# All tiles behind w_out lie 64 bytes further in SBUF, and the led expert's first-layer results begin at the first byte of their tiles

## The chip, the cores and the metric

The kernel runs on one core of one Trainium2 chip. The metric is the device time of one execution in microseconds (us). A core has five engines with queues of their own: TensorE (PE in the rows; its weight loads are listed as PEld), VectorE (DVE), ScalarE (ACT), GpSimd (POOL) and SyncE (SP, which here issues most DMAs). SBUF is the on-chip memory of 128 partitions; a tile has an address, the same in every partition, and the addresses below are bytes within a partition. PSUM takes the results of TensorE.

## The reference

```python
attn = sm_attn(mean4(q), mean4(k), mean4(v)) repeated 4x  +  local attention, |i - j| < 4    # 4 x 8 heads x 576 x 64
x = attn as [2304, 512]
h = maximum(maximum(x @ w1, x @ w2), x @ w3)          # [2304, 768]
x = h @ w_out                                         # [2304, 512]
e = argmax(x @ w_gate); g = softmax(x @ w_gate)[e]    # 8 experts, one per token
out = g * (relu(x @ W1[e]) @ W2[e])                   # 512 -> 1024 -> 512
```

## The kernel before

Every large product is made of three matmuls on parts: each operand is split into a high part (rounded to fp32r) and a low part (the rest), and high x high, low x high and high x low are accumulated in PSUM. The parts lie in SBUF as tiles of their own.

**Stages.** (1) Attention, in 16 units of two heads, to about 165 us; its results are the blocks `xb`, nine blocks of 256 tokens in four rotating tiles, each with a high and a low half. (2) The dense layers, block by block: `mul` (L1011, results `hp`) multiplies the weights w1, w2, w3 (stationary, 128x128 each, tiles `w{h,l}{n}`, shown as wh and wl) with `xb` (moving, 256 columns); 18 groups of 12 matmuls a block, 216 in all. The maximum of three goes to `ht` (tag `hT`, two rotating tiles). Then `mul_out` (L1039, results `yp`) multiplies `ht` (stationary) with `w_out` and the gate's columns (moving, 260 of 520 columns a matmul; tiles woh and wol); 72 matmuls a block. (3) Experts. The expert with most tokens (the led expert) is done in seven blocks of 256 tokens: `m1_led` (L1580, results `ehp`) has the expert's first layer as stationary operand, three of four parts in tiles of the tag `xb` (`ew1`), the fourth in pages that held w1 to w3 (`eh`, `el`), and the gathered tokens `xT` (tile `xL`) as moving operand; 96 matmuls a block. `relu_led` (L1592 on ScalarE, L1594 on VectorE) writes the results in two parts to two tiles `ehT` of the tag `hT`. `m2_led` (L1604, results `eo`) has `ehT` as stationary and the second layer `W2`, in pages, as moving operand, 512 columns; 48 matmuls a block. The other experts' full slots of 128 tokens follow: `m1` (L1687) with xT stationary and the first layer moving, `hte`, which writes `ehT` tiles of [128, 2, 8, 128] of the same tag `hT`, and `m2` (L1727), again `ehT` stationary and `W2` moving. The rests of fewer than 128 tokens (`racc`, L1849) are interleaved.

**Order of work.** A planner (`Plan`) with costs written by hand sets the order of every engine's instructions when the program is built. It knows durations and buffers, but no addresses.

**Where tiles lie.** Pools are stacks: a tag gets its place at its first `pool.tile`, in the order of the program, rounded up to 32 bytes. In the pool `main` these are the 18 weight pages of 4096 bytes, `lg` (576), the tag woh and the tag wol (12,480 bytes each, the size of the w_out tiles that take the place of `raw` and `tmp`), four tiles of the tag `xb` (8192 each), two of the tag `hT` (12,288 each), `hf`, `ys`. Behind `main` lies the pool of attention, and later in its place the pool `rt` of the experts (with `xL`). The identity `C["ident"]` lies in a pool ahead of `main`.

Of the kernel before, what the change touches and what calls it, by code (L numbers as in the profile page):

```python
# [10 lines left out]
F32 = mybir.dt.float32  # L11
F32R = mybir.dt.float32r
# [18 lines left out]
LED = 14  # L31
TB = 256
NB = NT // TB
OFF = 16
WIN, KW = 58, 64
NW = 10
CUT = (0, S // 2, S)
# [93 lines left out]
class Plan:  # L131
# [10 lines left out]
    def __init__(s, stock, fill=None, turns=()):  # L142
        s.fill, s.load, s.seen, s.cols = fill, 0.0, 0.0, [{} for _ in range(2)]
        s.stock = {k: [0.0] * n for k, n in stock.items()}
        s.jobs, s.free, s.port, s.turn, s.n = [], {}, 0.0, {t: [] for t in turns}, 0
# [134 lines left out]
class Attention:  # L280
# [36 lines left out]
    def bank(s, shape, name):  # L317
        return s.psum.tile(shape, F32, name=name, tag="at", bufs=4)
# [420 lines left out]
class Dense:  # L739


    def __init__(s, nc, pool, psum, ws, wo, wg, y, C):
        s.nc, s.pool, s.psum, s.ws, s.wo_d, s.wg_d, s.y, s.C = nc, pool, psum, ws, wo, wg, y, C
        s.hid, s.hp, s.hf, s.yp, s.ys, s.last, s.jl, s.js = {}, {}, {}, {}, {}, {}, [], []
        s.w = [[pool.tile([128, 2, 4, 128], F32R, name=f"w{i}", tag=f"w{i}{n}") for n in range(9)] for i in "hl"]
        s.xb = {}
        s.lg = pool.tile([128, NTL, E], F32, name="lg")
        s.ht, s.read = {}, {}

        s.raw = pool.tile([128, 3, 4, 128, 2], I32, name="raw", tag="woh")  # L750
        s.tmp = pool.tile([128, 3, 4, 128], F32, name="tmp", tag="wol")

    def bank(s, n, name):
        return s.psum.tile([128, n], F32, name=name, tag="mm", bufs=4)
# [305 lines left out]
class Experts:  # L1060
# [524 lines left out]
    def relu_led(s, f, part):  # L1585
        nc, t = s.nc, s.hp["led", f]
        if f + part == 0 and "led" not in s.hT:
            h = [s.pool.tile([128, OFF + 2048], F32R, name="ehT", tag="hT", bufs=2) for _ in range(2)]
            s.hT["led"] = [x[:, OFF:].rearrange("p (f t) -> p f t", f=8) for x in h]
        h, l = (x[:, f] for x in s.hT["led"])  # L1590
        if part == 0:
            nc.scalar.activation(out=h, in_=t, func=ACTF.Relu)  # L1592
        else:
            nc.vector.scalar_tensor_tensor(  # L1594
                out=l, in0=t, scalar=0.0, in1=h.bitcast(F32), op0=ALU.max, op1=ALU.subtract,
            )
# [433 lines left out]
```

## Time and profile before

| | |
|---|---|
| runs before | 696.35 us median of 3 (695.89 to 697.23) |
| profiled execution | 698.38 us, of which the span from the first to the last instruction is 696.5 us |
| PE busy | 680.4 us, 98% of the span |
| DVE, ACT, POOL busy | 346.1, 275.4, 126.7 us |
| granted TensorE clock | 0.995 of full speed as a mean |

Busy time of PE counts overlapping matmuls once; a matmul's own duration is longer than the distance from its start to the next start, because they are pipelined. The distance is read from how many matmuls begin in a stretch in which PE has no gap.

### The profile page before, as it was taken

To read this page: it belongs to the slowest core of one execution; us is meant where nothing else is said; L and a number is where in the kernel's file an instruction comes from. 1 tells how busy PE (TensorE), PEld (TensorE's weight loads), DVE (VectorE), ACT (ScalarE), POOL (GpSimd) and SP (SyncE) were. 2 spreads that over 40 slices of the span, in tenths; PEclk is the share of its full clock that TensorE was granted. 3 is DMA by queue.
4 is the path that set the end of the run, shared out by engine and by line. 5 is a ranking of instruction groups with operands and counts; after the bars stand their busy time and mean duration, and the time that the engine had idled before them with its cause. 6 is when DMAs were issued, how large, how long until landed. Compare 5 with 4: busy or idle time off the path is not lost.

```text
span 696.5 us, 15470 instructions
## 1 busy us (share of the span) xinstructions
PE 680.4 (98%) x6135; PEld 604.9 (87%) x6143; DVE 346.1 (50%) x849; ACT 275.4 (40%) x799; POOL 126.7 (18%) x148
## 2 busy tenths in 40 slices
PE   8898999999999999999999999999999999999996
PEld 4565799999999999999999999899898798787775
DVE  5989976796444472231222227864121121146863
ACT  3764656676453362222111112621221222237752
POOL 2436432302310020100000000412121211201111
PEclk9999999999999999999999999999999999999999
DMA  7756524334331110101000003605125343354640
GB/s 243 239 162 222 196 68 117 117 102 138 116 104 38 48 38 2 48 1 48 2 32 16 16 16 103 232 32 163 65 82 192 106 135 123 111 192 159 205 140 32
DMA packets 32241, 73.12 MB, mean 105 GB/s; under 512 B 4319, under 2 KB 4575, under 8 KB 32160
## 3 DMA queue, kind: packets, MB, share of 16 engines
q1 hardware_dynamic: 26528, 57.63, 25.7%
q0 software_dynamic: 3040, 9.70, 4.2%
q10 hardware_dynamic: 2592, 4.72, 1.9%
q8 instruction: 50, 0.82, 0.5%
q14 instruction: 31, 0.25, 0.1%
HBM read 75.18 MB, written 9.70 MB: 122 GB/s over the span
## 4 chain that ended last, share of the span: by engine, by line
PE 88%; DVE 5%; DMA 4%; issue 1%; SPq 1%; ACT 0%; POOL 0%; POOLq 0%; DVEq 0%; ACTq 0%
PE hp L1011 30%; PE ehp L1580 11%; PE yp L1039 11%; PE eo L1604 11%; PE eo L1727 3%; PE ehp L1687 3%; PE racc L1849 2%; PE tp L363 2%; PE to L568 1%; PE xtp L1672 1%; PE ts L398 1%; PE td L479 1%; PE tz L540 1%; DMA eh<-in_moe_w_dram 1%; PE tt L513 1%; DMA xg<-y,r_go 1%
## 5 line engine op out<-in xcount | busy, mean ns | idle before, releaser
L1011 PE MATMUL hp<-xb,wh 128*128 128x256 f32 x1296 | 230.8, 282 | 0.0
L1011 PEld LDWEIGHTS hp<-xb,wh 128*128 128x128 f32 x1296 | 196.2, 188 | 2.0 <-issue 0.8
L1011 PE MATMUL hp<-xb,wl 128*128 128x256 f32 x648 | 180.1, 278 | 0.0
L1011 PEld LDWEIGHTS hp<-xb,wl 128*128 128x128 f32 x648 | 121.9, 188 | 0.0
L1021 DVE TENSOR_TENSOR hf<-hf,hp 128x256 f32<-128x256 f32 x108 | 45.2, 419 | 93.3 <-PE hp L1011 91.6
L1594 DVE SCALAR_TENSOR_TENSOR ehT<-ehp,ehT 128x256 fp32r<-128x256 f32 x56 | 23.7, 424 | 114.1 <-ACT ehT L1592 113.9
L1604 PE MATMUL eo<-eh,ehT 128*128 128x512 f32 x224 | 69.9, 393 | 0.0
L1039 PE MATMUL yp<-woh,ht 128*128 128x260 f32 (+1 forms) x408 | 69.4, 290 | 0.0
L1580 PE MATMUL ehp<-xT,ew 128*128 128x256 f32 x504 | 68.7, 282 | 0.0
L1580 PEld LDWEIGHTS ehp<-xT,ew 128*128 128x128 f32 x504 | 63.1, 189 | 3.5 <-ACT ob L1739 1.7
L1024 ACT CAST ht<-hf 128x256 fp32r<-128x256 f32 x54 | 22.0, 407 | 94.4 <-DVE hf L1021 94.0
L1039 PEld LDWEIGHTS yp<-woh,ht 128*128 128x128 f32 x408 | 57.0, 188 | 1.0
L1604 PEld LDWEIGHTS eo<-eh,ehT 128*128 128x128 f32 x224 | 41.5, 188 | 10.7 <-issue 0.8
L1657 POOL DMA_INDIRECT xg<-y,r_go x14 | 17.6, 1254 | 165.8 <-DMA eh<-in_moe_w_dram 120.9
L1592 ACT ACTIVATE ehT<-ehp 128x256 fp32r<-128x256 f32 x56 | 21.5, 385 | 60.3 <-PE ehp L1580 60.3
L1604 PE MATMUL eo<-el,ehT 128*128 128x512 f32 x112 | 43.7, 390 | 0.0
L1039 PE MATMUL yp<-wol,ht 128*128 128x260 f32 (+1 forms) x204 | 43.2, 288 | 0.0
L1744 POOL DMA_INDIRECT out_dram<-ob,r_si x18 | 19.1, 1062 | 113.7 <-ACT ob L1739 101.9
L1739 ACT ACTIVATE ob<-eo,r_ga 128x512 f32<-128x512 f32 x17 | 11.7, 688 | 65.3 <-PE eo L1604 33.2
L1039 PEld LDWEIGHTS yp<-wol,ht 128*128 128x128 f32 x204 | 31.9, 188 | 0.5
L1028 DVE TENSOR_TENSOR ht<-hf,ht 128x256 fp32r<-128x256 f32 x54 | 23.6, 436 | 14.5 <-ACT ht L1024 14.1
L1018 ACT COPY hf<-hp 128x256 f32<-128x256 f32 x54 | 20.1, 372 | 25.6 <-PE hp L1011 25.5
(272 smaller groups left out, 1145.2 us busy)
## 6 DMA issues: line engine op xcount, KB each, us to landing
rw<-in_moe_w_dram SPq DMA_DIRECT2D x64, 256.0 KB
eh<-in_moe_w_dram SPq DMA_DIRECT2D x20, 512.0 KB
el<-in_moe_w_dram SPq DMA_DIRECT2D x20, 512.0 KB
raw<-in_moe_w_dram SPq DMA_DIRECT2D x18, 512.0 KB
vb<-in_vs_dram SPq DMA_DIRECT2D x16, 320.0 KB
qt<-in_q_dram SPq DMA_DIRECT2D x16, 288.0 KB
kt<-in_k_dram SPq DMA_DIRECT2D x16, 288.0 KB
vr<-in_v_dram SPq DMA_DIRECT2D x16, 288.0 KB
```

The lines of the kernel that those rows point to most:

```text
L1011: s.nc.tensor.matmul(t, s.part(a, m, g)[:, kk], s.xb[j][:, x, kk], start=n == 0, stop=n == 11)
L1018: s.nc.scalar.copy(out=s.hf[j, m], in_=s.hp.pop((j, m, 0)))
L1021: s.nc.vector.tensor_tensor(out=s.hf[j, m], in0=s.hf[j, m], in1=s.hp.pop((j, m, g)), op=ALU.max)
L1024: s.nc.scalar.copy(out=s.ht[j][:, 0, m], in_=s.hf[j, m])
L1028: s.nc.vector.tensor_tensor(out=h[:, 1, m], in0=s.hf.pop((j, m)), in1=h[:, 0, m].bitcast(F32), op=ALU.subtract)
L1039: s.nc.tensor.matmul(p, s.ht[j][:, a, kk, ts], s.wo[w][:, kk, c0:c1], start=kk + i == 0, stop=kk + i == 7)
L1580: s.nc.tensor.matmul(t, s.W1[j][a][:, f * 128:(f + 1) * 128], s.xL[:, x, j], start=n == 0, stop=n == 11,)
L1592: nc.scalar.activation(out=h, in_=t, func=ACTF.Relu)
L1594: nc.vector.scalar_tensor_tensor(out=l, in0=t, scalar=0.0, in1=h.bitcast(F32), op0=ALU.max, op1=ALU.subtract,)
L1604: s.nc.tensor.matmul(s.op[k, 0], h[a][:, j, i * 128:(i + 1) * 128], s.second(b, j), start=j == 0 and w == 0, stop=j == 7 and w == 2,)
L1687: s.nc.tensor.matmul(s.hp[k][f], a[:, j], s.W1[j][b][:, f * 512:(f + 1) * 512], start=j == 0 and w == 0, stop=j == 3 and w == 2,)
L1727: s.nc.tensor.matmul(s.op[k, cols.start], a[:, j], s.second(b, j, cols), start=j == 0 and w == 0, stop=j == 7 and w == 2)
```

## The change

A tile of 16 fp32 (64 bytes) that nothing reads or writes is allocated in the pool `main` right behind woh and wol, so every tile allocated after it (xb, hT, hf, ys, and the pools of attention and `rt`) lies 64 bytes further. The two `ehT` tiles of the led expert lose the 16 fp32 ahead of their results: they become plain [128, 8, 256] tiles. `ehT` of the slots (`hte`) had no such offset and is not edited.

```diff
-OFF = 16
+SHIFT = 16
...
         s.raw = pool.tile([128, 3, 4, 128, 2], I32, name="raw", tag="woh")
         s.tmp = pool.tile([128, 3, 4, 128], F32, name="tmp", tag="wol")
+        pool.tile([128, SHIFT], F32, name="shift")
...
     def relu_led(s, f, part):
         nc, t = s.nc, s.hp["led", f]
         if f + part == 0 and "led" not in s.hT:
-            h = [s.pool.tile([128, OFF + 2048], F32R, name="ehT", tag="hT", bufs=2) for _ in range(2)]
-            s.hT["led"] = [x[:, OFF:].rearrange("p (f t) -> p f t", f=8) for x in h]
+            h = [s.pool.tile([128, 8, 256], F32R, name="ehT", tag="hT", bufs=2) for _ in range(2)]
+            s.hT["led"] = h
         h, l = (x[:, f] for x in s.hT["led"])
```

## Rows read from the trace of the kernel before

**Rows 1.** The page: span, busy time of each engine, granted clock in 40 slices.
```profile
span 696.5 us, 15470 instructions
...
PE 680.4 (98%) x6135; PEld 604.9 (87%) x6143; DVE 346.1 (50%) x849; ACT 275.4 (40%) x799; POOL 126.7 (18%) x148
...
PEclk9999999999999999999999999999999999999999
```

**Rows 2.** The page: the chain that ended last, by engine and by line.
```profile
PE 88%; DVE 5%; DMA 4%; issue 1%; SPq 1%; ACT 0%; POOL 0%; POOLq 0%; DVEq 0%; ACTq 0%
PE hp L1011 30%; PE ehp L1580 11%; PE yp L1039 11%; PE eo L1604 11%; PE eo L1727 3%; PE ehp L1687 3%; PE racc L1849 2%; PE tp L363 2%; PE to L568 1%; PE xtp L1672 1%; PE ts L398 1%; PE td L479 1%; PE tz L540 1%; DMA eh<-in_moe_w_dram 1%; PE tt L513 1%; DMA xg<-y,r_go 1%
```

**Rows 3.** Busy time in two stretches: length, engines (instructions), clock, DMA share, GB/s.
```profile
293.00:308.00 15.00, 15.00 (x130) 15.00 (x129) 4.65 (x11) 3.23 (x9) 0.00 (x0) 1.00 0.00 1
321.00:340.00 19.00, 19.00 (x170) 19.00 (x169) 5.92 (x14) 3.44 (x9) 0.00 (x0) 1.00 0.00 1
```

**Rows 4.** L1011, 293.1 to 308, then 321 to 340: duration ns least/median/most.
```profile
L1011 PE MATMUL hp<-xb,wl x43: 280/281/282, 292.9 to 307.7; 128*128 128x256 f32 x43
L1011 PE MATMUL hp<-xb,wl x57: 275/276/277, 320.9 to 339.9; 128*128 128x256 f32 x57
```

**Rows 5.** Groups, blocks at 76:115, 117:163, 196:228, 238:273, 282:310, 318:343 (busy, mean ns).
```profile
L1011 PE MATMUL hp<-xb,wl 128*128 128x256 f32 x71 | 19.9, 280 | 0.0
L1011 PE MATMUL hp<-xb,wl 128*128 128x256 f32 x72 | 20.0, 278 | 0.0
L1011 PE MATMUL hp<-xb,wl 128*128 128x256 f32 x70 | 19.5, 278 | 0.0
L1011 PE MATMUL hp<-xb,wl 128*128 128x256 f32 x71 | 19.8, 279 | 0.0
L1011 PE MATMUL hp<-xb,wl 128*128 128x256 f32 x72 | 20.2, 280 | 0.0
L1011 PE MATMUL hp<-xb,wl 128*128 128x256 f32 x72 | 19.9, 277 | 0.0
```

**Rows 6.** The chain in order of time: start us, us on the chain, what.
```profile
291.77 18.37 PE hp L1011 x156
...
318.76 24.50 PE hp L1011 x216
343.26 8.62 PE yp L1039 x72
...
468.63 5.48 PE eo L1604 x24
...
505.10 11.24 PE ehp L1580 x96
...
531.13 11.45 PE ehp L1580 x96
...
649.91 5.71 PE eo L1727 x24
...
663.23 5.59 PE eo L1727 x24
...
684.37 5.67 PE eo L1727 x48
```

**Rows 7.** L1604 over the span, then L1727 from 661 to 667: least/median/most ns.
```profile
L1604 PE MATMUL eo<-eh,ehT x224: 387/389/500, 468.4 to 632.2; 128*128 128x512 f32 x112
L1727 PE MATMUL eo<-eh,ehT x12: 397/397/398, 663.1 to 666.8; 128*128 128x512 f32 x12
```

**Rows 8.** Busy time in a stretch of L1604 and one of L1727, columns as above.
```profile
470.00:475.00 5.00, 5.00 (x30) 4.29 (x28) 4.93 (x9) 0.00 (x0) 2.73 (x3) 1.00 0.38 105
661.50:666.50 5.00, 5.00 (x23) 4.07 (x22) 4.72 (x5) 4.11 (x5) 0.00 (x0) 1.00 0.00 0
```

## The prediction

> **What bounds the kernel now.** I read the page first, then the chain, then stretches of TensorE. The page shows PE busy for 680.4 of 696.5 us, with the granted clock at full speed in all 40 slices [rows 1], and the chain that ended last is 88% PE, 30% of it the three-way first layer (hp, L1011) [rows 2]. So nearly every nanosecond by which one matmul follows another counts, and the question for a change that only moves tiles is whether that spacing depends on where tiles lie. The reader should see in the rows that it does.
>
> Compare two stretches of one instruction. From 293 to 308 us PE runs 130 hp matmuls, from 321 to 340 us 170 of the same shape [rows 3]. On the chain, 156 of them take 18.37 us in the block around the first stretch, 117.8 ns each; 216 take 24.50 us in the next block, 113.4 ns each [rows 6]. The single matmul shows it too: 281 ns in the first stretch, with nothing outside 280 to 282, and 276 in the second, with nothing outside 275 to 277 [rows 4]. In both stretches PE never waits, the granted clock is 1.00, the DMA share is 0.00, and VectorE and ScalarE do much the same (4.65 and 3.23 us of 15; 5.92 and 3.44 of 19) [rows 3]. So neither clock nor DMA nor the other engines make the difference; what is left is how the two operands of TensorE are read beside each other, a pattern that, once entered, holds for 17 us.
>
> The same stands between two lines of one shape. The 128x512 second layer takes 389 ns at its median over all seven blocks of the led expert (L1604), and 397, nothing outside 397 to 398, in the slots behind it (L1727) [rows 7]; on the chain 24 of them take 5.48 us and 5.59 to 5.71 us, 228 and 233 to 238 ns each [rows 6]. Both read W2 from the same pages as the moving operand and an ehT tile as the stationary one. VectorE is as busy in the fast stretch (4.93 of 5 us) as in the slow one (4.72) [rows 8]. What differs is the place: the led expert's ehT begins 64 bytes into its tile, that of the slots at the first byte.
>
> **Distances.** I count, for each pair, moving start minus stationary start, modulo 512 bytes (one stationary block is 128 columns of 4 bytes, and inside every tile named here but those of w_out the slices start at multiples of 512). From the shapes in the order of allocation: 18 weight pages of 4096 bytes, lg of 576, woh and wol of 12,480 each make 99,264 bytes from the first page to xb, 448 modulo 512; the four xb tiles of 8192 and a 12,288-byte hT tile keep that, so hT lies at 448 as well, and xL at 384. Hence now: hp (moving xb, stationary pages) 448; led eo 448 + 64, so 0; slots' eo (stationary at 448) 64; ehp (moving xL) 448 against ew1, which lies in xb tiles, and 384 against its fourth weight part, which lies in pages. The rows say: 0 is fast, 64 slow, 448 either, and ehp at 448 with 384 is slow most of the time (96 in 11.24 to 11.45 us, 117 to 119 ns each) [rows 6].
>
> **The change part by part.** It adds a 64-byte tile that no instruction reads or writes, and takes the led expert's own 64 bytes away. No instruction, wait, DMA or queue entry is added, removed or moved past another; the planner's order doesn't depend on addresses. So only spacing can change.
>
> *Led eo (L1604):* pages stay, and ehT stays as well (64 bytes of shift in place of 64 of offset), so 0 remains: no change.
>
> *hp (L1011):* xb moves by 64, pages don't, so 448 becomes 0, the distance of led eo. What this is worth: a slow hp matmul costs 117.8 - 113.4 = 4.4 ns. How many are slow I read from the mean duration of the low-part matmuls by block: 280, 278, 278, 279, 280 in the first five and 277, which stands for the last four (276 to 277) [rows 5]. Over 277 the five are 3 + 1 + 1 + 2 + 3 = 10 ns; a wholly slow block would be 4 over it, so 2.5 blocks of 216 matmuls are slow: 540 x 4.4 ns = 2.4 us. Counted over 276 with 5 ns for a slow block it is 18/5 = 3.6 blocks, 3.4 us; I take 2.6. The first two blocks hold 4 of the 10 ns, and there attention is interleaved and waits of other engines set part of the end; half of their 1.0 us is lost. That leaves 2.1 us. Bounds: a gain of 3.4 where all becomes fast and all is on the path; a loss where all becomes slow (below).
>
> *Slots behind the led expert (L1727, L1687):* hT moves against W2's pages, so 64 becomes 0. On the chain the x24 pieces of 5.71, 5.59 and a third like it become 24 x 227 ns = 5.45 (0.26 + 0.14 + 0.14), and the x48 piece of 256 columns, 5.67 us, becomes 48 x 113.4 = 5.44 (0.23) [rows 6]: 0.77 us, of which I take 0.6, since this tail also waits on splits of VectorE and ScalarE (4.72 and 4.11 of 5 us [rows 8]). Bounds 0 and 0.77. Their first layer keeps its distance in three of four parts: nothing.
>
> *ehp (L1580):* ew1 and xL both move, so 448 stays; against pages 384 becomes 448. A quarter of the matmuls gets another distance. If all 672 ran at 113.4 ns, a block of 96 would take 10.89 us in place of 11.24 to 11.45, and the seven blocks would give 3.4 us; if all ran at 117.8 they would lose 0.3. I take the quarter, 0.8.
>
> *yp (L1039):* ht moves by 64 against woh and wol. These rows are 520 columns, so the distances run through 24 values in steps of 16 bytes and all of them shift together. A block of 72 takes 8.62 us, 119.7 ns each [rows 6], as a mean over fast and slow places; shifting the set of places leaves a mean much as it is. I take 0; 1 ns either way over some 600 is 0.6 us.
>
> *Attention:* its tiles move together, and only pairs with the identity, which stays, change. I take 0, and 1 us either way: tp is the longest of these lines on the chain, 2% of 696 us [rows 2], and 4 ns in 113 of that is 0.5.
>
> *DMAs:* the same packets to places 64 bytes on; 0.
>
> [...]
>
> **Sum.** 2.1 + 0.6 + 0.8 = 3.5 us. Against the profiled execution, 698.38 us with a span of 696.5 [rows 1], that is 694.9. The median of the runs is 696.35, 2.0 us lower with the same program; a pattern that holds by chance could be in fewer blocks there, so I take off some of it: 3.1 us, 693.2.
>
> **Rivals.** *Nothing happens.* hp at the one distance 448 runs at both paces, so distance alone doesn't decide; what starts the slow pattern may be the entry into a block, and then it comes and goes at 0 as well, while gains in the slots are eaten by yp. For it: the two paces in one tile. Against: led eo, whose median is 389 through seven blocks with many entries [rows 7]. 696.35, chance 0.18.
>
> *Slower: hp locks into the slow pattern at 0.* The slots' eo shows that a distance can be slow throughout, and no row shows a 256-column matmul at 0. Place: L1011, nine blocks. Of 1944 matmuls some 590 are slow now (2.6 us / 4.4 ns); the other 1354 would cost 4.4 ns each, 6.0 us, less 1.4 from slots and ehp: 696.35 + 4.6 = 701.0. It decides from some 330 additional slow matmuls on (1.4 us). [...] Chance 0.10.
>
> *More: ehp, all of it at one distance, locks into the fast pattern*, as hp did in four blocks: 2.1 + 0.6 + 3.4 = 6.1 us, 690.2. For it: hp's late blocks at 448. Against: hp's first five blocks at 448. Chance 0.12.
>
> **How the numbers follow.** My forecast, hp fast nearly throughout, slots fast, ehp partly, has 0.60, and 691.8 to 695.4 of its own. A measurement of this kernel can tell some 0.2%, 1.4 us. Faster by more than that: 0.57 of the forecast and all of the larger gain, 0.69. Within: 0.18 and 0.03, 0.21. Slower: 0.10. The range reaches from the larger gain to somewhat above no change, with yp and attention against it: 690.0 to 697.6; outside are the slow lock and the tails.
>
> **What would show it.** Right: hp low-part matmuls at 276 to 277 ns in all nine blocks, no stretch at 281, x216 pieces of 24.5 us; L1727 at 389 in place of 397; L1604 unchanged at 389; yp still near 8.6 us per 72. Wrong: hp at 281 in stretches or throughout, L1727 still at 397 (then distance modulo 512 is the wrong measure), or yp pieces moved by more than 0.1 us each. If hp is fast everywhere and the time stands, the gain went into waits in the attention part, and PE's idle time there would show it.

## The result, and the profile after

The changed kernel takes 705.0 us, the median of 5 runs (703.3 to 705.67), against 696.35 us for the kernel before on the same chip (695.77 to 697.36). The ratio is 1.0118, with a 95% interval of 1.0101 to 1.0136: it is slower by 8.65 us. The forecast was 693.2 us; the range ended at 697.6. What came is the rival to which the prediction gave 0.10, hp in the slow pattern at distance 0, and 4.0 us beyond its 701.0.

Behind the edit every line number is one higher than before: hp is L1012, the led expert's ehp L1581 and eo L1605, those of the slots L1688 and L1728.

The page of the changed kernel, to be read against [rows 1] and [rows 2]: span, busy time, granted clock, and the chain by line.

```profile
span 703.9 us, 15470 instructions
...
PE 689.5 (98%) x6135; PEld 612.9 (87%) x6143; DVE 346.3 (49%) x849; ACT 275.2 (39%) x799; POOL 126.0 (18%) x148
...
PEclk9999999999999999999999999999999999999999
...
PE hp L1012 34%; PE ehp L1581 11%; PE yp L1040 11%; PE eo L1605 11%; PE ehp L1688 3%; PE eo L1728 3%; PE racc L1850 2%; PE tp L363 2%; PE to L568 2%; PE td L479 1%; PE warm L1919 1%; PE xtp L1673 1%; PE tt L513 1%; PE tz L540 1%; PE ts L398 1%; PE tu L529 1%
```

The same instructions as before, 15470 of them, and the same granted clock, 0.9 or more of full speed in all 40 slices (mean 0.995 before, 0.996 now). PE is busy for 9.1 us more and stands idle for 14.4 us in place of 16.1, so the span is 7.4 us longer. On the chain only hp has a larger share of any weight, 34% in place of 30%.

Two stretches of hp in the changed kernel, as in [rows 3] (length, busy time and instructions of PE, PEld, DVE, ACT and POOL, clock, DMA share, GB/s).

```profile
296.00:311.00 15.00, 15.00 (x128) 15.00 (x127) 4.60 (x11) 2.74 (x7) 0.00 (x0) 1.00 0.01 1
325.00:344.00 19.00, 19.00 (x161) 19.00 (x160) 5.49 (x13) 3.12 (x8) 0.00 (x0) 1.00 0.00 1
```

Before, 19 us held 170 hp matmuls in the fast stretch; now they hold 161, with PE never idle, the clock at 1.00 and a DMA share of 0.00. The durations of the low-part matmul in these two stretches, as in [rows 4], and of the second layers as in [rows 7], with the last 256-column stretch of L1728 beside them (least, median and most ns):

```profile
L1012 PE MATMUL hp<-xb,wl x43: 283/283/284, 295.7 to 310.8; 128*128 128x256 f32 x43
L1012 PE MATMUL hp<-xb,wl x54: 282/284/284, 324.9 to 343.9; 128*128 128x256 f32 x54
...
L1605 PE MATMUL eo<-eh,ehT x224: 387/389/498, 477.3 to 640.0; 128*128 128x512 f32 x112
L1728 PE MATMUL eo<-eh,ehT x12: 389/389/390, 672.0 to 675.7; 128*128 128x512 f32 x12
L1728 PE MATMUL eo<-el,ehT x16: 279/283/284, 691.7 to 697.1; 128*128 128x256 f32 x16
```

There are no longer two paces in hp: both stretches stand at 283 to 284, above the 281 that was slow before. The 128x512 layers are both at 389, as the prediction said. The last row is the one that was missing before: the same pair of tiles at the same distance 0, but 256 columns wide, and it has 283, not 276.

The chain of the changed kernel in order of time (start us, us on the chain, what), the lines that answer to [rows 6] and the first and last pieces of the long layers:

```profile
78.39 3.07 PE hp L1012 x24
...
295.30 18.71 PE hp L1012 x156
314.01 8.63 PE yp L1040 x72
322.64 25.91 PE hp L1012 x216
...
417.63 8.63 PE yp L1040 x72
...
464.96 1.39 PE ehp L1581 x12
...
514.05 11.31 PE ehp L1581 x96
...
540.16 11.10 PE ehp L1581 x96
...
643.61 5.70 PE ehp L1688 x24
...
670.81 5.46 PE eo L1728 x24
...
691.65 5.76 PE eo L1728 x48
```

The landmarks of the chain of the kernel before that are needed to lay one chain on the other:

```profile
78.39 3.02 PE hp L1011 x24
...
409.50 8.62 PE yp L1039 x72
...
456.04 1.42 PE ehp L1580 x12
...
635.89 5.73 PE ehp L1687 x24
```

Both chains reach this hp piece of 24 at 78.39 us. From there the lag of the changed kernel is 3.87 us at the yp piece behind the fifth hp block (314.01 less the 310.14 at which the x156 piece of [rows 6] ends), 8.13 us at the yp piece behind the eighth (417.63 less 409.50: three whole blocks of 25.91 in place of 24.50, 1.41 each, make 4.23), and 8.92 us when the led expert begins (464.96 less 456.04). Then it falls: 7.72 us where the slots begin (643.61 less 635.89), 7.28 at the last piece (691.65 less 684.37). So hp costs 8.9 us, the led expert gives 1.2 back and the slots 0.4. This is the difference of the two profiled executions (705.67 and 698.38, 7.3 us); the medians differ by more because the profiled execution of before lay 2.0 us above its median and that of the changed kernel 0.7. The 24.50 us of a whole fast block is 113.4 ns for each of 216 matmuls, 25.91 is 119.95.

### The profile page after: what moved, and what is told of

Same layout as the page of the kernel before. It is cut to its first block, busy times and chain, and to the rows that moved or that the text cites. A ratio compares the mean times of both kernels' runs of the same rounds, so it can differ in the third digit from the quotient of the medians.

```text
span 703.9 us, 15470 instructions
## 1 busy us (share of the span) xinstructions
PE 689.5 (98%) x6135; PEld 612.9 (87%) x6143; DVE 346.3 (49%) x849; ACT 275.2 (39%) x799; POOL 126.0 (18%) x148
## 4 chain that ended last, share of the span: by engine, by line
PE 92%; DVE 4%; DMA 2%; ACT 1%; issue 0%; SPq 0%; POOLq 0%; ACTq 0%
PE hp L1012 34%; PE ehp L1581 11%; PE yp L1040 11%; PE eo L1605 11%; PE ehp L1688 3%; PE eo L1728 3%; PE racc L1850 2%; PE tp L363 2%; PE to L568 2%; PE td L479 1%; PE warm L1919 1%; PE xtp L1673 1%; PE tt L513 1%; PE tz L540 1%; PE ts L398 1%; PE tu L529 1%
## 5 line engine op out<-in xcount | busy, mean ns | idle before, releaser
L1012 PE MATMUL hp<-xb,wh 128*128 128x256 f32 x1296 | 240.0, 287 | 0.0
L1012 PEld LDWEIGHTS hp<-xb,wh 128*128 128x128 f32 x1296 | 201.4, 192 | 1.9 <-issue 0.8
L1012 PE MATMUL hp<-xb,wl 128*128 128x256 f32 x648 | 183.5, 283 | 0.0
L1012 PEld LDWEIGHTS hp<-xb,wl 128*128 128x128 f32 x648 | 124.1, 192 | 0.0
L1605 PE MATMUL eo<-eh,ehT 128*128 128x512 f32 x224 | 69.9, 393 | 0.0
L1581 PE MATMUL ehp<-xT,ew 128*128 128x256 f32 x504 | 67.9, 280 | 0.0
L1581 PEld LDWEIGHTS ehp<-xT,ew 128*128 128x128 f32 x504 | 62.4, 188 | 3.5 <-ACT ob L1740 1.7
L1605 PEld LDWEIGHTS eo<-eh,ehT 128*128 128x128 f32 x224 | 41.5, 188 | 10.8 <-issue 0.8
L1605 PE MATMUL eo<-el,ehT 128*128 128x512 f32 x112 | 43.7, 390 | 0.0
```

The lines of the kernel that those rows point to most:

```text
L1012: s.nc.tensor.matmul(t, s.part(a, m, g)[:, kk], s.xb[j][:, x, kk], start=n == 0, stop=n == 11)
L1581: s.nc.tensor.matmul(t, s.W1[j][a][:, f * 128:(f + 1) * 128], s.xL[:, x, j], start=n == 0, stop=n == 11,)
L1605: s.nc.tensor.matmul(s.op[k, 0], h[a][:, j, i * 128:(i + 1) * 128], s.second(b, j), start=j == 0 and w == 0, stop=j == 7 and w == 2,)
```

## The experiments

First theory: the distance between the starts of the two operands sets the pace, as the prediction had it, but 0 is a slow distance for 256 columns. Rivals: the address itself counts, not the distance; or something else that moved 64 bytes (attention, yp, DMAs) took the time. The letters in the expectations are names of theories and their variants; the words behind each run say what held. Each time is the median of 4 to 12 runs, each ratio is to the kernel before on the same chip, with its 95% interval.

### One half of the change each

The shift alone, with the 64 bytes of the led expert's ehT kept (hp to 0, led eo to 448):

```
+        pool.tile([128, 16], F32, name="shift")
```

> The 64-byte tile alone; the led expert's ehT keeps its 64-byte offset, so its results begin 64 bytes further than before. Theory A (the distance between moving and stationary operand, modulo 512 bytes, sets the spacing, and 256 columns at distance 0 are slow): hp at 283 ns as in the changed kernel, eo of the led expert (336 matmuls, now at distance 448) no longer at 0 and likely slower by up to 5 ns each, 1.7 us: 705.0 to 706.7. Rival B (the offset's removal is what costs): about 696.4, hp as before.

Measured: 705.12 us, ratio 1.0132 (1.0105 to 1.016), theory A's number. The offset alone, without the shift (hp stays at 448, led eo to 64):

```
-OFF = 16
+OFF = 0
```

> The 64-byte tile is left out, the led expert's results begin at the first byte of their tiles. Theory A: hp as before (mixed 276 and 281 ns); eo of the led expert at distance 64, as the slots behind it had: 397 in place of 389 ns, 336 x 5 ns = 1.7 us: 698.0. Rival B: about 705.

Measured: 696.41 us, ratio 1.001 (0.9998 to 1.0022): B fell, and A's 698.0 is too high. The chains of both kernels in order of time, the shift alone first:

```profile
321.37 25.91 PE hp L1012 x216
...
489.49 10.90 PE ehp L1581 x96
501.26 11.21 PE eo L1605 x48
...
538.89 11.09 PE ehp L1581 x96
```

```profile
317.83 24.50 PE hp L1011 x216
...
492.38 11.01 PE eo L1604 x48
...
662.40 5.59 PE eo L1727 x24
```

The shift brings the whole loss, with the 25.91 of the changed kernel to the hundredth. The offset was worth far less than expected: led eo at 64 takes 11.01 us per 48, against 10.91 to 10.93 at 0, some 0.1 us for each of seven blocks. At 448 it takes 11.21. In the kernel with the offset alone the slots' eo, at 64 as well, takes 5.59 us per 24, or 232.9 ns, where the led expert's has 229.4: for 512 columns too, one distance shows two paces.

And ehp, wholly at 448 in the first of the two, is fast in all six whole pieces of the chain: 10.90 us twice (113.5 ns), then 11.08 to 11.09. The last four of these six pieces hold some 0.2 us more in the kernel before as well, and that is not the pace: there the single matmul has 281 ns at its median in a piece of 11.24 and in one of 11.45 alike. The changed kernel, with the same distance, is slow in the first two (11.31, 281 ns) and fast in the last four (11.10 to 11.11, 276 ns).

### Distance or address

A 64-byte tile ahead of the weight pages moves every one of the tiles named, and all distances stay:

```
+        pool.tile([128, 16], F32, name="shift0")
         s.w = [[pool.tile(...
```

> The kernel before, with the 64-byte tile ahead of the weight pages: pages, w_out, xb, hT and all behind move together by 64 bytes, so every distance stays and every address changes. Theory A: hp mixed as before, 696.4 within 1.5 us. Rival C (the absolute place of xb, not the distance, sets the spacing): hp at 283 ns, 704 to 705.

Measured: 695.94 us, ratio 0.9999 (0.9984 to 1.0013): A held, C fell. The 64 bytes put between xb and hT, so that hp keeps 448 and the slots' eo comes to 0:

```
+        if not j:
+            s.pool.tile([128, 16], F32, name="shift2")
...
-OFF = 16
+OFF = 0
```

> The 64-byte tile between xb and hT, the offset left out: xb and the pages keep their places, hT, hf, ys and the pools behind move. Theory A: hp mixed as before; the led expert's first layer (ehp) goes to distance 0 against its three parts in xb tiles, so 504 of its 672 matmuls turn slow (283 ns, 120 ns apart, from 117): +1.5 us; slots' eo at 389 in place of 397, -0.6 us: about 697.3. Rival D (moving hT or the pools behind it is what costs): about 704, with hp at 283 ns.

Measured: 697.22 us, ratio 1.0023 (1.0008 to 1.0037): A held, D fell. The chain of the kernel with everything moved, then of the one with the tile behind xb:

```profile
315.96 24.50 PE hp L1012 x216
```

```profile
316.67 24.50 PE hp L1013 x216
...
503.18 11.46 PE ehp L1582 x96
...
662.26 5.45 PE eo L1729 x24
...
683.11 5.76 PE eo L1729 x48
```

With xb and everything behind it at other addresses, hp keeps 24.50: for this step of 64 bytes the address doesn't count. With hp's distance kept, 64 bytes behind it cost 1.1 us, and that has its own pair: ehp, now at 0 in three parts of four, takes 11.46 in its first two whole pieces (119.4 ns), where it had 11.27 and 11.24, and 11.65 to 11.66 in the last four, where it had 11.42 to 11.45, so some 0.2 us more in each. The slots' eo at 0 shows both shapes in one kernel: 24 of 512 columns in 5.45 us (227 ns, fast), 48 of 256 in 5.76 (120 ns, slow).

### Other distances for hp

Which distances are free for 256 columns? Six layouts, each by tiles of a few words that nothing reads (SHIFT behind wol, shift3 ahead of xL), by ehT's own offset OFF, and by lg or raw (woh) allocated ahead of the weight pages in place of behind them. hp at 480:

```
-OFF = 16
+OFF = 0
...
+        pool.tile([128, 8], F32, name="shift")
...
+        s.rt.tile([128, 8], F32, name="shift3")
```

> A 32-byte tile in place of the 64-byte one, a second one ahead of xL, no offset: hp at distance 480, ehp at 480 (three parts) and 448 (one), eo of the led expert and the slots at 32. Theory A (256 columns have a free stretch of distances with its edge at 448, between 384 and 512): if the free side is this one, hp and ehp run at 276 to 277 ns throughout, -2.5 us each, eo between the 389 of distance 0 and the 397 of 64, up to +1 us: 691 to 692.5. Rival E (every distance but 448 is slow for 256 columns): hp and ehp at 283 ns, +9 and +1.8 us: 706 to 708.

Measured: 705.21 us, ratio 1.0126 (1.01 to 1.0152), a little under the 706 to 708 of rival E and far from theory A: 32 bytes are enough to do the harm. hp at 416:

```
-OFF = 16
+OFF = 32
...
+        s.lg = pool.tile([128, NTL, E], F32, name="lg")
         s.w = [[pool.tile(...
...
+        pool.tile([128, 8], F32, name="shift")
...
+        s.rt.tile([128, 24], F32, name="shift3")
```

> The tile lg ahead of the weight pages in place of behind them, and a 32-byte tile behind w_out: hp at 416; ehp at 32 (three parts) and 448 (one); eo of the led expert at 480 by an offset of 128 bytes, the slots' at 96. Theory A: if the free side is this one, hp at 276 to 277 ns throughout, -2.5 us; ehp at 32, next to the slow 0, at 281 to 283, +1.5; eo at 480, next to the slow 448, 392 to 397, up to +1.7; sum 695 to 697. Rival E: hp at 283 ns, +9 us: 705 to 708.

Measured: 704.88 us, ratio 1.0123 (1.0094 to 1.0152), at the edge of rival E: 416 is slow too. hp at 384, with lg ahead of the pages, OFF = 96 and 32 words for shift3:

> The tile lg ahead of the weight pages: hp at 384; ehp at 64 and 448; eo of the led expert at 256 by an offset of 384 bytes, the slots' at 128. Theory A: 384 was slow for the fourth part of ehp (119 ns of spacing at its median), so hp is slow throughout: +7 to +9 us; ehp at 64 slow, +1; eo at 256 unknown, 0 to +2: 704 to 708. Rival F (the free stretch lies below 448 and is at least 64 bytes wide): hp at 276 ns, 693 to 697.

Measured: 702.5 us, ratio 1.0086 (1.0061 to 1.011), a little under theory A's figure; 384 is not free, so F fell. hp at 32, with 24 words for shift and OFF = 16 kept:

> A 96-byte tile in place of the 64-byte one, the 64-byte offset kept: hp at 32; ehp at 448 (three parts) and 480 (one); eo of the led expert at 416, the slots' at 480. Theory A: hp slow as at 0, 281 to 283 ns, +7 to +9 us; ehp mixed or fast, 0 to -2.5; eo at 416 slow as at 448 (394 to 400 ns), +2: 702 to 707. Rival G (0 alone, at which both operands start in the same place of 512 bytes, is slow for 256 columns, and any step off it frees them): hp at 276 ns, 694 to 697.

Measured: 701.9 us, ratio 1.0073 (1.0045 to 1.0102), at the edge of theory A: G fell. hp at 320, which is 448 less 128:

```
-OFF = 16
+OFF = 48
...
+        s.raw = pool.tile([128, 3, 4, 128, 2], I32, name="raw", tag="woh")
         s.w = [[pool.tile(...
...
+        pool.tile([128, 16], F32, name="shift")
```

> The first tile of w_out (tag woh) ahead of the weight pages, and the 64-byte tile of the change: hp at distance 320; eo of the led expert at 0 by an offset of 192 bytes; ehp at 448 and 256, slots' eo at 192. Theory H, from the runs so far (256 columns repeat every 128 bytes: 64, 448 fastest with 114 to 115 ns of spacing, 0 and 384 slowest with 118 to 120): 320 is 64 modulo 128, so hp at 276 to 277 ns at its median, total as before, 695 to 698. Rival I (64 and 448 are special, the pattern doesn't repeat): hp at 281 to 283 ns, 701 to 706.

Measured: 701.54 us, ratio 1.008 (1.0064 to 1.0096), rival I's range: H fell. hp at 256, the same without the shift tile and with OFF = 64:

> The same without the 64-byte tile: hp at 256; ehp at 448 and 192, both 64 modulo 128; eo of the led expert at 0, the slots' at 256. Theory H: hp slow as at 0 and 384, 281 to 283 ns, +7 to +9 us; ehp fast, 114 to 115 ns of spacing, -1.5 to -2 us; slots' 512-column matmuls at 389 ns, -0.4 us: 701 to 704. Rival J (what is fast for 512 columns at 256 is so for 256 columns too): hp at 276 ns, 691 to 694.

Measured: 703.11 us, ratio 1.0095 (1.0076 to 1.0115): 256 is slow for 256 columns, and J fell. Lines of the chains of the kernels with hp at 480, 416, 384, 32, 320 and 256, one fence each:

```profile
319.21 25.55 PE hp L1012 x216
...
498.13 11.20 PE eo L1606 x48
```

```profile
318.05 25.34 PE hp L1012 x216
```

```profile
320.20 25.64 PE hp L1011 x216
...
486.73 10.98 PE ehp L1581 x96
498.58 10.93 PE eo L1605 x48
...
688.08 5.71 PE eo L1728 x48
```

```profile
319.01 25.21 PE hp L1012 x216
```

```profile
316.66 25.44 PE hp L1012 x216
...
686.11 5.46 PE eo L1728 x48
```

```profile
320.09 25.92 PE hp L1011 x216
...
667.74 5.46 PE eo L1727 x24
...
688.58 5.75 PE eo L1727 x48
```

Together with the rows above (a piece of the chain by its count gives the ns; hp is a whole late block, eo the first piece of 48 of the led expert):

| distance | 256 columns, hp x216: us, ns | 512 columns, eo x48: us, ns |
|---|---|---|
| 0 | 25.91, 120.0 | 10.92, 227.5 |
| 32 | 25.21, 116.7 | 11.20, 233.3 |
| 64 | 24.91, 115.3 (nearly all pages; first attempt below) | 11.01, 229.4 |
| 256 | 25.92, 120.0 | 10.93, 227.7 |
| 320 | 25.44, 117.8 | |
| 384 | 25.64, 118.7 | |
| 416 | 25.34, 117.3 | 11.25, 234.4 (kernel with hp at 32) |
| 448 | 24.50, 113.4 | 11.21, 233.5 |
| 480 | 25.55, 118.3 | 11.20, 233.3 (kernel with hp at 416) |

The two shapes have different free places, the places where the fast pace was seen: 512 columns run free at 0 and 256, 256 columns at 448 and at none of the seven others tried for all of hp. That 0 and 256 agree in both columns speaks for a period of 256 bytes, and so does 128, at which the last eo of the kernel with hp at 384 has 119.0 ns (5.71 us per 48), beside 118.7 at 384. A period of 128 fell with hp at 320, where 448 would have had its like. In that kernel the last eo, 256 columns at 192, took 5.46 us per 48, 113.8 ns: 192 is 448 less 256, and free there too.

At 64 the rows differ among themselves: hp has 115.3 ns; ehp, with three parts of four at 64, took 10.98 per 96 (114.4 ns) in the kernel with hp at 384; and the slots' x48 piece at 64 before took 5.67 (118.1 ns) [rows 6]. So 64 and 320, which also lie 256 apart, neither bear out the period (115.3 against 117.8 in hp) nor refute it.

### Two attempts at a better layout

If each shape gets its free place, the kernel should gain. The first attempt keeps ehp at 448 and all eo of 512 columns at 0, and pays with hp at 64 for nearly all pages (the fifth page of either part goes last, with 64 bytes more; the slots' ehT gets the led expert's offset):

```
-OFF = 16
+OFF = 112
...
+            if n == 4:
+                t = pool.tile([128, 1024 + 16], F32R, name=f"w{i}", tag=f"w{i}{n}")
...
+            x = s.pool.tile([128, OFF + 2048], F32R, name="ehT", tag="hT", bufs=2)
+            s.hT[k] = x[:, OFF:].rearrange("p (i f t) -> p i f t", i=2, f=8)
```

> Every 256-column product at 64 modulo 128: the two pages that later hold the fourth first-layer part of the led expert are allocated last and are 64 bytes longer, so dense weights and this part lie 64 bytes apart in them; hp at 64 and 448, ehp at 448 throughout, eo of the led expert and of the slots at 0 by offsets of 448 bytes. Theory H: hp at 114 to 115 ns of spacing as before, ehp 114 in place of 117, -2 us; slots' 512-column matmuls 389 in place of 397 ns, -0.3 us: 693.5 to 694.5. Rival K (the slow pattern is entered by chance at any of these distances): hp and ehp mixed as before, 695.5 to 697.

Measured: 698.63 us, ratio 1.0036 (1.0022 to 1.0049): slower than both ranges, a miss; each whole late block of hp takes 0.41 us more at 64 (24.91). The second puts all 256-column pairs at 192 modulo 256 and all 512-column pairs at 0 modulo 256:

```
+            if n == 4:
+                t = pool.tile([128, 1024 + (48, 16)[x]], F32R, name=f"w{i}", tag=f"w{i}{n}")
...
+        s.rt.tile([128, 16], F32, name="shift3")
...
+            o = 2 * OFF if k == NS1 - 1 else OFF
+            x = s.pool.tile([128, o + 2048], F32R, name="ehT", tag="hT", bufs=2)
```

> Each product at the distance where its shape was fastest in the runs so far: 256 columns at 192 modulo 256 (hp as before; ehp at 448 in all four parts, by 64 bytes ahead of xL and by the fourth part lying 192 bytes off its page's start; the last slot's two 256-column halves at 192), 512 columns at 0 modulo 256 (eo of the led expert and of the slots). One small tile shares another's place to make room. Theory L (distance modulo 256, with a free place of its own for each width): hp spaced 114 to 115 ns, ehp 114 to 115 in place of 117 (-1.3 to -2.1 us), slots' 512 columns at 389 in place of 397 ns and the last halves at 276 (-0.5 us): 693.5 to 694.5. Rival K (at 192 the slow pattern is entered by chance, and hp in its nine blocks may lose what ehp gains): 695.5 to 698.

Measured: 695.68 us against 696.31, ratio 0.999 (0.9978 to 1.0002): not told apart from before, in the range of rival K and not in that of theory L. The chain of the first attempt, then of the second:

```profile
318.34 24.91 PE hp L1019 x216
```

```profile
318.21 24.50 PE hp L1019 x216
...
480.60 11.31 PE ehp L1591 x96
...
530.25 11.11 PE ehp L1591 x96
...
607.44 11.50 PE ehp L1591 x96
...
661.29 5.46 PE eo L1740 x24
...
682.14 5.67 PE eo L1740 x48
```

The 512-column pieces are free (5.46 per 24), and hp's late blocks are. But ehp at its free place is fast in only three of its six whole pieces: 11.31 twice (117.8 ns), then 11.10 to 11.11 three times, then 11.50 (in the changed kernel 11.31 went with single matmuls of 281 ns and 11.10 to 11.11 with 276), where the shift alone was fast in all six at the same 448. And the last eo, 256 columns at 192, takes 5.67 per 48 where the kernel with hp at 320 had 5.46. hp's late blocks have 113.4 ns at 448 and at 192 and at no other distance tried, so the distance sets what is within reach; but the other lines show that a free place alone doesn't bring the fast pace. No layout that ran is shown to beat the kernel before.

## Why the prediction was wrong

**What bounds it** was right: PE at full clock (0.995 as a mean) and nearly without waits (98% of the span busy), so that the time follows from how closely matmuls follow each other, and that from where tiles lie. With the shift alone no operation is added or removed, and a block of hp takes 25.91 us in place of 24.50. That it is the distance and not the address is shown by the kernel with everything moved by 64 bytes, which keeps 24.50. That the cause is how the two operands are read beside each other was the prediction's inference: the runs show how the spacing goes with the distance, and not what happens in the reading.

**The step that failed** is hp: "448 becomes 0, the distance of led eo". It took a distance that rows showed fast for 128x512 to be fast for 128x256. As the prediction says under its slower rival, no row showed a 256-column matmul at 0. The changed kernel shows both shapes at distance 0 on one line, L1728: 389 ns at 512 columns, and 283 at 256, where the fast pace has 276. hp was to give 2.1 us and cost 8.9.

**Why 8.9 and not more.** Had all 1944 hp matmuls gone from a mix of 1354 at 113.4 and 590 at 117.8 ns, the prediction's count, to 119.95, that would be 8.9 + 1.3 = 10.1 us. The first five blocks, in which attention is interleaved, lag by only 3.87 us; by the same count all five would lose 5 x 216 x 6.55 ns less 590 x 4.4 ns, 4.5 us. So by this count 0.6 us of the 4.5 did not reach the end, much as the prediction's caution about the early blocks had it (it took off 0.5); that waits are the reason is not shown. The ninth, beside the router, lags by 0.8 us and not by 1.4. The slow rival, at 701.0, had place and sign right; it priced the slow pace by the 117.8 of [rows 6], the only slow pace there was to see, and 0 is slower still. The difference of 2.15 ns on 1944 matmuls, 4.2 us, is about what its price lacked (8.65 less 4.6).

**Led eo, 0:** right, 389 ns [rows 7] and 10.91 to 11.13 us per 48.

**Slots, 0.6 us:** half right. The 512-column pieces went from 5.71 and 5.59 to 5.67 and 5.46 [rows 6]. The first of them holds some 0.2 us beyond its pace in the changed kernel as well, so the 0.26 counted on it could not come: its single matmuls had medians of 388 and 394 ns in the two parts, not 397, and have 390. The x48 piece of 256 columns, which was to fall by 0.23, rose from 5.67 to 5.76, by the same mistake as hp. On the chain 0.4 us.

**ehp, 0.8 us:** right in sign and nearly in size, in part by luck: the led expert gave 1.2 us. It came as whole blocks and not as a quarter of every block: four pieces went from 11.42 to 11.45 to 11.10 to 11.11, and the two ahead of them became slower by 0.04 and 0.07 (to 11.31). The working also took the step from 11.24 to 11.45 for a change of pace, which it is not (281 ns in both). So 3.4 us was too high a bound: with all six whole pieces fast, the shift alone gains 2.1 us on them. Nor does "lose 0.3" follow: seven blocks of 96 at 117.8 ns are 79.2 us, and seven at the middle of 11.24 and 11.45 are 79.4. What is open is why the same distance, 448 for all four parts, gives six, four or three fast pieces, with the shift alone, in the changed kernel and in the second layout.

**yp, attention, DMAs, 0:** right as far as seen; yp is at 8.63 us per 72 against 8.62, both chains reach hp at 78.39 us, and PE's idle time fell from 16.1 to 14.4 us.

**The chances.** "0 is fast, 64 slow, 448 either" was read from rows of two shapes as if they were one. The rows of 281 and 276 ns lie at one distance, so they spoke for two paces and not for the place; only 389 against 397 spoke for the place. For 256 columns the rows showed 448 at both paces, 64 slow (the slots' x48 piece, 118.1 ns) and 384 in a quarter of ehp, and none of the distances tried since was better for hp than 448; a move to a distance that no row of that shape shows deserved more than 0.10 on the slow side.

What stays open: what decides which pace is entered at the free place (for 256 columns 448 shows both in hp's early blocks and in ehp, 192 both in the last eo; for 512 columns 64 shows 229.4 and 232.9), how the distance acts inside TensorE, and why the free places of 256 and 512 columns differ.

## What to carry to other kernels

Where TensorE runs back to back at full clock, compare the spacing of matmuls of one shape between stretches; if it differs by a few per cent (here 117.8 against 113.4 ns in one kernel, 119.95 in the changed one) with no wait, DMA or clock beside it, look at where the two operands begin. Here 64 bytes that nothing reads cost 1.3% by shifting one operand against the other (705.12 us against 696.08), so after any edit of allocations look at the spacing again before explaining the time by the edit itself. Carry a distance from one line to another only if the shape is the same: at 0 matmuls of 512 columns had their fast pace here (227.5 ns) and those of 256 columns a slow one (120.0).

## What the runs showed of the hardware

The spacing of matmuls went with the distance of the two operands' starts: 128x256 from 113.4 ns (448) to 120.0 ns (0 and 256), 128x512 from 227.5 ns (0; 227.7 at 256) to 234.4 ns (416). A period of 256 bytes fits the pairs 0 and 256 (120.0 ns both for 256 columns), 128 and 384 (119.0 and 118.7), 192 and 448 (113.8 and 113.4, and slower too at both); 64 and 320 (115.3 and 117.8) leave it open.

The records of the weight loads don't tell the slow pace. Over the span, the group of hp's loads, whose mean was 188 ns before, has 192 at distance 0 (the changed kernel, the first line), and 188 still at 480 (the second), where hp takes 118.3 ns:

```profile
L1012 PEld LDWEIGHTS hp<-xb,wl 128*128 128x128 f32 x648 | 124.1, 192 | 0.0
```

```profile
L1012 PEld LDWEIGHTS hp<-xb,wl 128*128 128x128 f32 x648 | 122.1, 188 | 0.0
```

In hp's late blocks a pace held for whole blocks of 216 matmuls (three of 24.50 us each before, three of 25.91 in the changed kernel); from one block of ehp to the next it changed (11.31 us per 96 to 11.11 and, in the last block, 11.50, in the second layout). Steps of 32 bytes already matter (113.4 ns at 448, 118.3 at 480).
